# Expert 0's working memory at the other end of SBUF, a hand-given order for all engines from the end of attention on, Sinkhorn steps issued in thirds, and three of x's differences on GpSimd

## The chip, the core and the metric

The kernel runs on one core of a Trainium2 chip. The metric is the device time of one execution in microseconds; the median of three runs is given. Names of engines: PE is TensorE, DVE is VectorE, ACT is ScalarE, POOL is GpSimd, SP the queue from which all transfers here are issued.

## What is computed

Sliding-window attention with four sink positions, then a mixture of experts whose weights P come from a Sinkhorn normalisation over all tokens (cut from the reference):

```python
keep = is_sink | in_window                       # 4 sinks, window 128, B=4, H=8, S=768, D=64
a = softmax(where(keep, scale * q @ k.T, -1e9)); x = (a @ v) as (3072, 512)

logits = x @ w_gate; logits = logits - logits.max(); P = np.exp(logits)      # 3072 x 8
for _ in range(8):
    P /= P.sum(1, keepdims=True) + 1e-09
    P /= P.sum(0, keepdims=True) + 1e-09
    P *= N / E
for e in range(E):                               # E = 8, x 512 wide, hidden 1024
    out += P[:, e:e + 1] * (np.maximum(x @ w1[e], 0.0) @ w2[e])
```

## The kernel before

Every float32 operand of a large product is held as two pieces, a rounded one (made by ACT) and the rest (made by DVE from the raw value and the rounded one); a product is then three matmuls. `split` and `piece` make such pairs.

**Attention** (to about 322 us) runs over 48 units (batch, block of 128 tokens, half of the heads). Its PE order is written by hand; the order of the other engines is the scheduler's. In the gaps PE works on expert 0 for the first 1024 tokens (`plain`, L614, called through `run_fill`): one step of it is half of a first product (six 256-column matmuls, L587) or a third of a second product (three 512-column matmuls, L603). 36 of its 128 steps are left when attention ends. x goes to DRAM as `xscr`.

**Between attention and the table-driven part.** The remaining 36 steps are issued (L692 to L696) with the first five calls of the generator `sinkhorn` (L22) between them. Each of its eight iterations has a DVE part (row sums, reciprocal, multiplication, column sums), a small PE product that adds the column sums over the partitions (L49) and another DVE part. Then x's four blocks of 512 tokens by 256 columns are loaded (`load_x`, L917), four differences T1 to T4 of blocks are formed (`make_form`, L928, all four on DVE here) and split; then come the weight units of experts 1 to 7, numbered n, each 256 hidden columns wide (28 in all). A unit has seven first products M1 to M7 (`first`, six matmuls each, L721) and, one unit later, eight second products (`second`, six matmuls each, L993), in the order `STEPS`, where `S_` is a second product:

```python
STEPS = ["M2", "M1", "M5", S_, "M3", S_, "M6", S_, S_, "M7", S_, S_, "M4", S_, S_]
```

For a unit the raw weights r1 and r2 are loaded, sums of r1 formed on POOL (`sums1`, L781), and r1, the sums and r2 split into W1f and W2f; all of it goes to DRAM too, for the other two thirds of the tokens.

**What sets the order.** Units 0 to 2 (`AUTO = 3`) are left to the scheduler, with Sinkhorn's steps at high priority between them; from unit 3 on a table (`plan`) says at which step every engine's work stands. When Sinkhorn is done, expert 0's eight results are multiplied by its weights on DVE (L1013). The buffers of r1 and r2 (`rawp0`) lie where expert 0's work lay: its pools `wa`, `rawp` and `hp` share one end of SBUF with the attention's, and the next pools of that end follow when they close.

After unit 27 two more passes over the other tokens follow, from the stored pieces; they are not touched.

Of the kernel before, what the change touches and what calls it, by code (L numbers as in the profile page):

```python
# [16 lines left out]
P = 128  # L17
# [4 lines left out]
def sinkhorn(nc, pool, psum, Lt, Pt, ident, ones, NT, E, N):  # L22

    Lf = Lt.rearrange("p t e -> p (t e)")
    Pf = Pt.rearrange("p t e -> p (t e)")
    m1 = pool.tile([P, 1], F32, name="m1")
    nc.vector.reduce_max(m1, Lf, axis=AX.X)
# [10 lines left out]
    nc.scalar.activation(Pf, Lf, AF.Exp, bias=nm)  # L38
    for _ in range(8):
        r = pool.tile([P, NT], F32, name="rsum")  # L40
        nc.vector.reduce_sum(r, Pt, axis=AX.X)
        nc.vector.tensor_scalar(r, r, 1e-9, None, op0=ALU.add)
        nc.vector.reciprocal(r, r)
        nc.vector.tensor_tensor(Pt, Pt, r.unsqueeze(2).broadcast_to([P, NT, E]), op=ALU.mult)
        c = pool.tile([P, E], F32, name="csum")
        nc.vector.reduce_sum(c, Pt.rearrange("p t e -> p e t"), axis=AX.X)
        yield
        cb = psum([P, E])
        nc.tensor.matmul(cb, lhsT=ones, rhs=c, start=True, stop=True)  # L49
        c2 = pool.tile([P, E], F32, name="csum2")  # L50
        nc.vector.tensor_scalar(c2, cb, 1e-9, None, op0=ALU.add)
        nc.vector.reciprocal(c2, c2)
        nc.vector.scalar_tensor_tensor(Pt, Pt, float(N / E), c2.unsqueeze(1).broadcast_to([P, NT, E]), op0=ALU.mult, op1=ALU.mult)

# [25 lines left out]
def tile_any_span(ctx: ExitStack, tc: tile.TileContext, q, k, v, span, wg, w1, w2, out):  # L80
# [82 lines left out]
    with ExitStack() as ph:  # L163
# [5 lines left out]
        Lt = gp.tile([P, NT, E], F32, name="g_lt")  # L169
        Pt = gp.tile([P, NT, E], F32, name="g_pt2")  # L170
        for t in range(NT):
# [49 lines left out]
def tile_sink_attention_moe(ctx: ExitStack, tc: tile.TileContext, q, k, v, wg, w1, w2, out):  # L221
# [86 lines left out]
    Lt = const.tile([P, NT, E], F32, name="Lt")  # L308
    Pt = const.tile([P, NT, E], F32, name="Pt")
# [38 lines left out]
    with ExitStack() as ph:  # L348
        psg1 = ph.enter_context(tc.tile_pool(name="psg1", bufs=1, space=PSUM))
        pso1 = ph.enter_context(tc.tile_pool(name="pso1", bufs=1, space=PSUM))  # L350
        ps_s = ph.enter_context(tc.tile_pool(name="ps_s", bufs=2, space=PSUM))
        ps_t = ph.enter_context(tc.tile_pool(name="ps_t", bufs=2, space=PSUM))
        ps_o = ph.enter_context(tc.tile_pool(name="ps_o", bufs=2, space=PSUM))
# [3 lines left out]
        XF["B12"] = wa.tile([P, 2, KH, HT], F32R, name="B12", bufs=1)  # L357
        ab = ph.enter_context(ExitStack())
        att = ab.enter_context(tc.tile_pool(name="att", bufs=2))
        att1 = ab.enter_context(tc.tile_pool(name="att1", bufs=1))  # L360

        SS = []
        for j in range(2):
            s = att1.tile([P, SK], F32R, name=f"SS{j}")
            nc.vector.tensor_copy(s, zero[:, 0:SK])
            SS.append(s)

        KT = []
        for hh in range(2):
            t = att1.tile([P, 2, NP, (NB + 1) * SEG], F32R, name=f"KT{hh}")  # L370
            for w in range(2):
                for pr in range(NP):
                    nc.vector.tensor_copy(t[:, w, pr, SINK:SEG], zero)
            KT.append(t)

        units = [(b, i, hh) for b in range(B) for i in range(NB) for hh in range(2)]
        us = {}
        seq = {}
        raws = {}
        later, gates = [], []  # L380
# [48 lines left out]
        def split_v(n):  # L429
# [6 lines left out]
            if i == 0:  # L436
                split_sinks(b, hh)
# [60 lines left out]
        def values(n, pr):  # L498
# [15 lines left out]
            if pr == NP - 1:  # L514
                store_x(n)
# [921 lines left out]
```

## Time and profile before

| | us |
|---|---|
| median of 3 runs | 2194.5 (2192.27 to 2194.94) |
| the profiled execution | 2192.53, its span 2190.8 |
| PE busy in the span | 2152.2 (98%) |
| DVE, ACT, POOL busy | 1564.5, 888.4, 739.6 |
| mean granted clock of TensorE, as a share of full speed | 0.996 |

The page puts 93% of the span's chain of waits on PE. Busy time is counted in modelled matmul spans, so what a stretch is worth is read from how many matmuls it finished and at which granted clock (1.00 is 2.4 GHz, 0.50 is 1.2 GHz). The stretch that the change touches lies between 322 us (end of attention) and 421 us (first step of unit 3).

### The profile page before, as it was taken

The numbers are of one execution on the slowest core, as the hardware profiler recorded it, in microseconds if no ns is written. First come the engines' busy times: TensorE is split into PE (matmuls) and PEld (weight loads), VectorE is DVE, ScalarE is ACT, GpSimd is POOL, SyncE is SP. The second block draws the span as 40 slices with busy tenths as digits, with TensorE's granted clock in tenths as the row PEclk, the third lists the DMA queues.
The fourth block names the chain that finished last, engine by engine and source line by source line (L and its number), as shares of the span: only waits on it lengthen the run. The fifth ranks groups of instructions, "written<-read, shape, count | busy, mean of one in ns | idle before, by whom it ended". The sixth has DMA issues, their size and how long they took to land.

```text
span 2190.8 us, 31969 instructions
## 1 busy us (share of the span) xinstructions
PE 2152.2 (98%) x10525; PEld 1776.9 (81%) x10525; DVE 1564.5 (71%) x2913; ACT 888.4 (41%) x1906; POOL 739.6 (34%) x957
## 2 busy tenths in 40 slices
PE   7999998999999999999999999999999999999998
PEld 5888886788888888878888888888788888888886
DVE  8878868777778777776666666666756666666666
ACT  7777753344444444433333322233342333323222
POOL 7655542232332332232223332222322222332322
PEclk9999998999999999999999999999999999999999
DMA  7333324689988998876666666667866666666662
GB/s 175 83 84 87 81 76 149 199 294 289 315 294 289 308 305 288 279 274 220 193 201 202 199 201 202 201 193 231 310 211 201 203 199 193 202 205 192 202 194 82
DMA packets 396636, 454.89 MB, mean 208 GB/s; under 512 B 99696, under 2 KB 263728, under 8 KB 395568
## 3 DMA queue, kind: packets, MB, share of 16 engines
q1 hardware_dynamic: 396464, 452.77, 66.0%
q8 instruction: 86, 1.41, 0.3%
q14 instruction: 86, 0.70, 0.1%
HBM read 315.21 MB, written 137.46 MB: 207 GB/s over the span
## 4 chain that ended last, share of the span: by engine, by line
PE 93%; DVE 4%; ACT 1%; issue 1%; POOL 0%; DMA 0%; SPq 0%; DVEq 0%; POOLq 0%; ACTq 0%
PE c L721 39%; PE o L1284 20%; PE held L1284 8%; PE o L993 7%; PE held L993 7%; PE O L513 3%; PE ps L456 2%; PE g L587 2%; PE pt L477 2%; PE o L603 1%; PE pt L417 1%; PE O L603 1%; ACT sc L462 1%; PE ps L587 0%; PE O L543 0%
## 5 line engine op out<-in xcount | busy, mean ns | idle before, releaser
L747 ACT CAST hf<-w 128x512 fp32r<-128x512 f32 x448 | 265.7, 621 | 564.2 <-POOL w L1251 301.1
L1284 PE MATMUL o<-hf,W2q 128*128 128x512 f32 x1920 | 476.2, 392 | 0.1
L1284 PEld LDWEIGHTS o<-hf,W2q 128*128 128x128 f32 x1920 | 360.5, 188 | 78.1 <-DVE acc L1295 0.5
L721 PE MATMUL c<-T,W1q 128*128 128x512 f32 x1530 | 388.6, 389 | 0.0
L748 DVE TENSOR_TENSOR hf<-w,hf 128x512 fp32r<-128x512 f32 x448 | 330.2, 765 | 71.0 <-ACT hf L747 62.6
L721 PEld LDWEIGHTS c<-T,W1q 128*128 128x128 f32 x1530 | 287.0, 188 | 60.9 <-ACT M L1228 0.4
L1295 DVE TENSOR_TENSOR acc<-o,acc 128x512 f32<-128x512 f32 x300 | 206.3, 688 | 176.5 <-PE o L1284 176.1
L721 PE MATMUL c<-B,W1q 128*128 128x512 f32 x1134 | 278.5, 390 | 0.0
L1251 POOL TENSOR_TENSOR w<-w 128x512 f32<-128x512 f32 x64 | 83.1, 1298 | 500.9 <-DVE w L1233 492.3
L721 PEld LDWEIGHTS c<-B,W1q 128*128 128x128 f32 x1134 | 212.6, 188 | 44.8
L1232 DVE TENSOR_TENSOR w<-c,M 128x512 f32<-128x512 f32 x192 | 132.3, 689 | 143.0 <-PE c L721 138.4
L1228 ACT COPY M<-c 128x512 f32<-128x512 f32 x192 | 112.7, 587 | 252.9 <-PE c L721 252.2
L1284 PE MATMUL held<-hf,W2q 128*128 128x512 f32 x768 | 196.5, 392 | 0.0
L721 PE MATMUL c<-T,W1f 128*128 128x512 f32 x672 | 173.2, 394 | 0.4 <-DVE C L965 0.4
L993 PE MATMUL o<-W2f,h 128*128 128x512 f32 x672 | 171.5, 391 | 0.8 <-DVE acc L1000 0.8
L993 PE MATMUL held<-W2f,h 128*128 128x512 f32 x672 | 172.0, 390 | 0.0
L1284 PEld LDWEIGHTS held<-hf,W2q 128*128 128x128 f32 x768 | 144.2, 188 | 30.7
L1266 POOL TENSOR_TENSOR w<-w 128x512 f32<-128x512 f32 x64 | 105.6, 1650 | 177.6 <-DVE hf L748 177.6
L721 PEld LDWEIGHTS c<-T,W1f 128*128 128x128 f32 x672 | 127.1, 190 | 28.9 <-DVE C L965 1.2
L993 PEld LDWEIGHTS o<-W2f,h 128*128 128x128 f32 x672 | 126.1, 188 | 28.6 <-DVE acc L1000 1.2
L993 PEld LDWEIGHTS held<-W2f,h 128*128 128x128 f32 x672 | 126.1, 188 | 26.5
L1255 POOL TENSOR_TENSOR w<-w 128x512 f32<-128x512 f32 x64 | 83.7, 1308 | 176.0 <-DVE w L1233 174.6
(198 smaller groups left out, 3081.3 us busy)
## 6 DMA issues: line engine op xcount, KB each, us to landing
W2q<-w2s SPq DMA_DIRECT2D x448, 256.0 KB
W1q<-w1s SPq DMA_DIRECT2D x444, 256.0 KB
w1s<-W1f SPq DMA_DIRECT2D x56, 896.0 KB
w2s<-WT SPq DMA_DIRECT2D x136, 256.0 KB
r<-in_moe_w_dram SPq DMA_DIRECT2D x64, 512.0 KB
w2s<-W2f SPq DMA_DIRECT2D x56, 256.0 KB
PB<-psd SPq DMA_DIRECT2D x16, 512.0 KB
w2s<-W2f SPq DMA_DIRECT2D x56, 128.0 KB
```

Source lines behind the costliest of these rows:

```text
L513: nc.tensor.matmul(u["O"][:, pr], lhsT=x_, rhs=y_, start=(j == 0), stop=(j == len(ops) - 1))
L721: nc.tensor.matmul(ps, lhsT=w1(a, k), rhs=x[:, b, k, :], start=(start and j == 0), stop=(stop and j == len(TERMS) - 1), skip_group_check=n ...
L747: nc.scalar.copy(dst[:, 0], src)
L748: at(1, lambda: nc.vector.tensor_sub(dst[:, 1], src, f32(dst[:, 0])))
L993: nc.tensor.matmul(o, lhsT=h[c, th][:, a, off:off + P], rhs=W2F[n][:, w, c, :], start=(begin and c == 0 and j == 0), stop=(end and c == 1 ...
L1228: nc.scalar.copy(t, T["c2"])
L1232: nc.vector.tensor_add(w, T["c1"], T[m])
L1251: nc.gpsimd.tensor_sub(S3, T["A11"], T["A21"])
L1255: nc.gpsimd.tensor_add(T["A21"], T["A21"], T["A22"])
L1266: at(k, lambda: nc.gpsimd.tensor_sub(T["A11"], w, T["A11"]))
L1284: nc.tensor.matmul(o, lhsT=W2Q[part, n, m][:, a, k * P:(k + 1) * P], rhs=F[part, n, H_OF[m]][:, w, :], start=(j == 0 and (begin or not hol ...
L1295: nc.vector.tensor_add(sums[m, k], o, sums[m, k])
```

## The change

1. **Memory.** Expert 0's buffers (hidden values, second weights, x's block B12, first weights and raw weights) are taken from the right end of SBUF, attention's from the left. The left pools for units 0 and on are opened at once when attention ends, and wait tile by tile. Unit n's odd hidden values and all W2f continue in expert 0's buffers. x's block (1,0) is loaded into B12's.
2. **Order.** From the end of attention on, all engines stand in the order of a table: 28 steps (`REST`), each with one step of expert 0, then the units from 0 on, `plan` now with rows for units 0 to 2. The last eight steps of expert 0 are the `S_` of unit 0. Unit 0's second products take the held banks first. The second pieces of w2 of units 0 to 2 that were loaded again later (`job_w2`) are made in units 1 and 2.
3. **Sinkhorn.** An iteration is three calls instead of one; the additions of 1e-9 (two DVE instructions in each iteration) are replaced by an extra column and row of the tile that hold 1e-9. The rows of the table place the 27 calls: 13 in REST, 6 in unit 0, 8 in unit 1.
4. **Engines.** T1, T3 and T4 are formed on POOL (T2 on DVE); expert 0's results are weighted on ACT.

Loads at the end of attention on SP, before and after (x10 is block (1,0); r1 and r2 are raw weights of units in order):

```order
L527 DMA xscr_121<-xr_5239 128x4x128
L922 DMA x10_5599<-xscr_121 128x2x512
L922 DMA x00_5601<-xscr_121 128x2x512
L922 DMA x01_5603<-xscr_121 128x2x512
L922 DMA x11_5605<-xscr_121 128x2x512
L770 DMA r1_5635<-in_moe_w1_dram 128x4x256
L775 DMA r2_5637<-in_moe_w2_dram 128x2x512
L770 DMA r1_5824<-in_moe_w1_dram 128x4x256
```

```order
L538 DMA xscr_120<-xr_5244 128x4x128
L921 DMA x00_5351<-xscr_120 128x2x512
L921 DMA x01_5353<-xscr_120 128x2x512
L775 DMA r1_5355<-in_moe_w1_dram 128x4x256
L921 DMA x11_5357<-xscr_120 128x2x512
L780 DMA r2_5359<-in_moe_w2_dram 128x2x512
L775 DMA r1_5361<-in_moe_w1_dram 128x4x256
L775 DMA r1_5595<-in_moe_w1_dram 128x4x256
L921 DMA B12_5632<-xscr_120 128x2x512
```

The first raw weights stand between x's blocks, and block (1,0) has moved behind three units' r1, into B12's buffer.

PE where expert 0's steps end and unit 0 begins, before and after (ps and O are expert 0's first and second products, csum goes into a Sinkhorn product, c1 and c2 are unit 0's):

```order
L603 MATMUL O_5526<-W2_3793,h0_5397 128x512 x6
L49 MATMUL pt_5533<-csum_5488,ones_74 128x8
L603 MATMUL O_5526<-W2_3803,h1_5454 128x512 x6
L49 MATMUL o_5671<-csum_5544,ones_74 128x8
L721 MATMUL c2_5662<-B21_125,W1f_5644 128x512 x4
L721 MATMUL c1_5684<-B11_124,W1f_5644 128x512 x4
L721 MATMUL c2_5662<-B21_125,W1f_5644 128x512 x2
L49 MATMUL o_5695<-csum_5682,ones_74 128x8
L721 MATMUL c1_5684<-B11_124,W1f_5644 128x512 x2
```

```order
L56 MATMUL pt_5573<-csum_5538,ones_74 128x8
L598 MATMUL ps_5579<-B12_156,W1_3805 128x256 x2
L598 MATMUL ps_5579<-B22_125,W1_3805 128x256 x2
L598 MATMUL ps_5579<-B12_156,W1_3805 128x256 x2
L614 MATMUL O_5550<-W2f_3808,h11_5404 128x512 x3
L598 MATMUL ps_5579<-B22_125,W1_3805 128x256 x2
L598 MATMUL ps_5579<-B12_156,W1_3805 128x256 x2
L598 MATMUL ps_5579<-B22_125,W1_3805 128x256 x2
L614 MATMUL O_5550<-W2f_3808,h11_5404 128x512 x3
L725 MATMUL c2_5634<-B21_124,W1f_5448 128x512 x6
L56 MATMUL held1_5643<-csum_5606,ones_74 128x8
L725 MATMUL c1_5648<-B11_123,W1f_5448 128x512 x6
```

Expert 0 has eight steps left when unit 0 begins, and a Sinkhorn product stands at fixed places in PE's queue.

DVE at the same place, before and after (T and W1f rows make the rest pieces, rsum, csum and the Pt or Xt rows are Sinkhorn's, h is a hidden value's rest piece, acc a result of expert 0):

```order
L342 TENSOR_TENSOR T1_5609<-x00_5601,T1_5609 128x2x256
L51 TENSOR_SCALAR csum2_5673<-o_5671 128x8
L342 TENSOR_TENSOR T3_5616<-x01_5603,T3_5616 128x2x256
L52 RECIPROCAL csum2_5673<-csum2_5673 128x8
L342 TENSOR_TENSOR T3_5616<-x01_5603,T3_5616 128x2x256
L53 SCALAR_TENSOR_TENSOR Pt_120<-Pt_120,csum2_5673 128x192
L342 TENSOR_TENSOR T2_5623<-x11_5605,T2_5623 128x2x256
L41 TENSOR_REDUCE rsum_5677<-Pt_120 128x24
L342 TENSOR_TENSOR T2_5623<-x11_5605,T2_5623 128x2x256
```

```order
L752 TENSOR_TENSOR T2_5548<-x11_5357,T2_5548 128x2x256 x2
L604 SCALAR_TENSOR_TENSOR h01_5540<-ps_5541,h01_5540 128x256
L58 RECIPROCAL csum2_5575<-pt_5573 128x8
L59 SCALAR_TENSOR_TENSOR Xt_119<-Xt_119,csum2_5575 128x24x8
L752 TENSOR_TENSOR W1f_5448<-ST_5447,W1f_5448 128x512 x2
L48 TENSOR_REDUCE rsum_5592<-Xt_119 128x24
L49 RECIPROCAL rsum_5592<-rsum_5592 128x24
L604 SCALAR_TENSOR_TENSOR h01_5540<-ps_5579,h01_5540 128x256
L51 TENSOR_TENSOR Xt_119<-Xt_119,rsum_5592 128x24x8
L53 TENSOR_REDUCE csum_5606<-Xt_119 128x8
L622 TENSOR_TENSOR acc_3724<-O_5550,acc_3724 128x512
```

Unit 0's W1f now stands on DVE among expert 0's last steps, and T3 and T4 behind unit 0's first products. The diff, cut to its core:

```diff
-def sinkhorn(nc, pool, psum, Lt, Pt, ident, ones, NT, E, N):
+def sinkhorn(nc, pool, psum, X, ident, ones, NT, E, N):
...
     for _ in range(8):
         r = pool.tile([P, NT], F32, name="rsum")
-        nc.vector.reduce_sum(r, Pt, axis=AX.X)
-        nc.vector.tensor_scalar(r, r, 1e-9, None, op0=ALU.add)
+        nc.vector.reduce_sum(r, X[:, 0:NT, :], axis=AX.X)
         nc.vector.reciprocal(r, r)
+        yield
         nc.vector.tensor_tensor(Pt, Pt, r.unsqueeze(2).broadcast_to([P, NT, E]), op=ALU.mult)
         c = pool.tile([P, E], F32, name="csum")
-        nc.vector.reduce_sum(c, Pt.rearrange("p t e -> p e t"), axis=AX.X)
+        nc.vector.reduce_sum(c, X[:, :, 0:E].rearrange("p t e -> p e t"), axis=AX.X)
         yield
         cb = psum([P, E])
         nc.tensor.matmul(cb, lhsT=ones, rhs=c, start=True, stop=True)
         c2 = pool.tile([P, E], F32, name="csum2")
-        nc.vector.tensor_scalar(c2, cb, 1e-9, None, op0=ALU.add)
-        nc.vector.reciprocal(c2, c2)
+        nc.vector.reciprocal(c2, cb)
...
+    p0r = ctx.enter_context(ExitStack())
+    right = lambda stack, name, bufs: stack.enter_context(tc.tile_pool(name=name, bufs=bufs, reuse_waits="tile", side="right"))
+    hpr, w2pr, b12p = right(p0r, "hpr", 1), right(p0r, "w2pr", 2), right(p0r, "b12", 1)
...
-        wa = ph.enter_context(tc.tile_pool(name="wa", bufs=2))
-        rawp = ph.enter_context(tc.tile_pool(name="rawp", bufs=2))
-        hp = ph.enter_context(tc.tile_pool(name="hp", bufs=2))
+    wa, rawp = right(ph, "wa", 2), right(ph, "rawp", 2)
...
-            for k_ in (2, 12, 10, 10, 8):
-                with tc.high_priority():
-                    next(sk)
-                run_fill(k_)
-            for _ in fill:
-                pass
...
         def sinkhorn_step():
-                    for t in range(TH):
-                        nc.vector.tensor_scalar(acc[t], acc[t], Pt[:, t, 0:1], None, op0=ALU.mult)
+            for k, t in enumerate((4, 6, 0, 2, 5, 7, 1, 3)):
+                at(k + 1, lambda t=t: nc.scalar.activation(acc[t], acc[t], AF.Copy, scale=Pt[:, t, 0:1]))
...
+        for j, ks in {0: (), 1: ((0, (0, 1, 4, 7, 10, 3)), (1, (5, 6, 8, 11, 12, 9)))}.get(n, ((n, (0, 1, 3, 6, 9, 5)),)):
...
+            todo[12 if n == 1 else 2].append(lambda: load2(n + 1))
...
+        if n < 2:
+            for k in ((1, 2, 3, 6, 7, 8), (0, 1, 1, 4, 5, 5, 8, 8))[n]:
+                todo[k].append(sinkhorn_step)
+        if n == 0:
+            form_steps(todo, {"T3": (4, 5), "T4": (7, 9)})
+            todo[0].append(lambda: load_x(0, (1, 0)))
+            todo[3].append(lambda: make_form("T4", nc.gpsimd))
...
+    REST = 28
+    load_x(0, (0, 0), (0, 1))
+    load1(0)
+    load_x(0, (1, 1))
+    load2(0)
+    load1(1)
+    for k in (0, 2, 4, 6, 10, 12, 13, 17, 19, 20, 24, 26, 27):
+        todo[k].append(sinkhorn_step)
+    for k, f in ((7, lambda: make_form("T1", nc.gpsimd)), (12, lambda: make_form("T3", nc.gpsimd)),
+                 (17, lambda: sums1(0)), (18, lambda: make_form("T2")), (23, lambda: sums1(1)),
...
+    form_steps(todo, {"T1": (14, 15), "T2": (21, 22)})
+    for k in range(REST):
+        tick(lambda: [f() for f in todo[k]], lambda: next(fill))
```

## Rows read from the trace of the kernel before

**Rows 1.** The page's busy times: us (share of span) and instructions of each engine.

```profile
PE 2152.2 (98%) x10525; PEld 1776.9 (81%) x10525; DVE 1564.5 (71%) x2913; ACT 888.4 (41%) x1906; POOL 739.6 (34%) x957
```

**Rows 2.** Stages: stretch, length; busy us (instructions) by engine; granted clock, DMA share, GB/s.

```profile
322.20:348.50 26.30, 26.30 (x158) 22.87 (x156) 16.22 (x41) 7.39 (x16) 0.00 (x0) 1.00 0.19 65
348.50:352.40 3.90, 0.56 (x3) 0.30 (x2) 3.87 (x11) 0.09 (x1) 0.00 (x0) 1.00 0.67 207
352.40:360.70 8.30, 3.96 (x9) 2.94 (x10) 8.30 (x13) 3.83 (x8) 8.11 (x8) 0.71 0.65 230
360.70:369.50 8.80, 8.12 (x20) 5.71 (x19) 6.68 (x17) 4.27 (x8) 0.03 (x1) 0.50 0.89 304
369.50:420.65 51.15, 47.48 (x207) 37.34 (x207) 40.36 (x77) 15.88 (x30) 11.06 (x12) 1.00 0.68 220
420.65:900.00 479.35, 479.35 (x2104) 394.81 (x2103) 360.88 (x549) 217.38 (x403) 151.88 (x184) 1.00 0.89 292
```

**Rows 3.** PE in order of time: start, us, instructions, count [idle before].

```profile
322.20 0.87 PE L587 MATMUL ps<-B,W 128*128 128x256 f32 x6
...
420.65 2.92 PE L721 MATMUL c<-B,W1f 128*128 128x512 f32 x12
```

**Rows 4.** Whom PE waited for, 322 to 421 us: total, times, longest.

```profile
PE c L721 <- DVE W1f L342: 3.8, 1, 3.8
PE o L49 <- DVE csum L46: 2.2, 1, 2.2
PE o L1022 <- DVE pe L1017: 2.1, 1, 2.1
```

**Rows 5.** Whom SP's queue waited for, 319 to 352 us.

```profile
SPq L770 <- DVE h L593: 20.3, 1, 20.3
```

**Rows 6.** SP in order of time: x's loads, first raw weights.

```profile
319.39 3.44 SPq L922 DMA_DIRECT2D x<-xscr  x4
348.73 0.37 SPq L770 DMA_DIRECT2D r<-in_moe_w_dram  x1
```

**Rows 7.** DVE in order of time: one Sinkhorn iteration with POOL idle.

```profile
339.71 0.42 DVE L593 SCALAR_TENSOR_TENSOR h<-ps,h 128x256 fp32r<-128x256 f32 x1 [1.86 <-ACT h L592]
340.06 0.17 DVE L51 TENSOR_SCALAR csum<-pt 128x8 f32<-128x8 f32 x1
340.26 0.20 DVE L52 RECIPROCAL csum<-csum 128x8 f32<-128x8 f32 x1
340.50 0.36 DVE L53 SCALAR_TENSOR_TENSOR Pt<-Pt,csum 128x192 f32<-128x192 f32 x1
340.89 0.35 DVE L41 TENSOR_REDUCE rsum<-Pt 128x24 f32<-128x192 f32 x1
...
341.49 0.30 DVE L43 RECIPROCAL rsum<-rsum 128x24 f32<-128x24 f32 x1
341.82 0.36 DVE L44 TENSOR_TENSOR Pt<-Pt,rsum 128x192 f32<-128x192 f32 x1
342.22 0.52 DVE L46 TENSOR_REDUCE csum<-Pt 128x8 f32<-128x192 f32 x1
```

**Rows 8.** DVE in order of time: four of x's differences, POOL idle.

```profile
328.20 1.89 DVE L932 TENSOR_TENSOR x<-x,x 128x512 f32<-128x512 f32 x3
...
331.62 0.68 DVE L932 TENSOR_TENSOR x<-x,x 128x512 f32<-128x512 f32 x1
```

**Rows 9.** DVE's groups by shape, 352.4 to 360.7 us, POOL busy: count, us, mean ns.

```profile
L342 DVE TENSOR_TENSOR T<-x,T 128x512 fp32r<-128x512 f32 x5 | 4.5, 898 | 0.0
L342 DVE TENSOR_TENSOR W1f<-r,W1f 128x512 fp32r<-128x512 f32 x1 | 1.2, 1207 | 0.0
L53 DVE SCALAR_TENSOR_TENSOR Pt<-Pt,csum 128x192 f32<-128x192 f32 x1 | 0.9, 884 | 0.0
L44 DVE TENSOR_TENSOR Pt<-Pt,rsum 128x192 f32<-128x192 f32 x1 | 0.9, 878 | 0.0
```

**Rows 10.** POOL in order of time: a later form's difference, two halves.

```profile
923.13 3.38 POOL L932 TENSOR_TENSOR x<-x,x 128x512 f32<-128x512 f32 x2 [1.23 <-DVE x L932]
```

More of the change, by code (lines that the diff above doesn't have):

```diff
@@ L542, in gate_tile, with gate_step, load_plain, plain_g1 @@
+    def gate_step():
+        if gates and next(gates[0], 0) == 0:
+            gates.pop(0)
+            gate_step()
+    def load_plain(e, u):
+        r1, r2 = load_raw(rawp, e, u)
+        W1 = wa.tile([P, 2, KC, UF], F32R, name="W1")
+        split(W1, r1)
+        W2 = w2pr.tile([P, 2, 2, DM], F32R, name="W2f")
+        split(W2, r2)
+        return W1, W2
+    def plain_g1(W, u, c, h, g, th):
+        ps = bank1([P, GH])
+        i = 0
+        for a, w in ((0, 0), (0, 1), (1, 0)):
             for kc in range(KC):
-                nc.tensor.matmul(lg, lhsT=xr[:, kc, :], rhs=wg_raw[:, kc, :], start=(kc == 0), stop=(kc == KC - 1))
@@ L708, in tile_sink_attention_moe @@
+    ab.close()
     early.close()
@@ L733, in at @@
     def at(steps, f):
+        assert steps > 0
         due.setdefault(clock[0] + steps, []).append(f)
@@ new lines, in store, with store_unit, small @@
+    def store(dst, i, src):
+        for w in range(2):
+            nc.sync.dma_start(dst[:, i:i + src.shape[2] // HD, w], f32(src[:, w]).rearrange("p (a c) -> p a c", c=HD))
+    def store_unit(n):
+        e, u = units0[n]
+        kept(e, u)
+        store(w1s[e, u], 0, W1F[n].rearrange("p w a k f -> p w (a k f)"))
+        store(w2s[e, u], 0, W2F[n][:, :, 0, 0:HD])
+        store(w2s[e, u], 1, W2F[n][:, :, 1])
+    def small(n_):
+        return wtp.tile([P, 2, 2 * HD], F32R, name="WT")[:, :, 0:n_]
@@ new lines, in jobs, with load_x @@
+    def jobs():
+        units = [job_unit(0, u) for u in range(NU)]
+        xs = [job_x(2, q) for q in range(4)]
+        for j in range(NU):
+            yield from units[j]
+            yield from xs[j]
+    raw = {}
+    def load_x(part, *blocks):
+        for kh, th in blocks:
+            r = raw[f"B{kh + 1}{th + 1}"] = xraw(f"x{kh}{th}")
+            t0 = part * NPART + th * HT
+            nc.sync.dma_start(r, xscr[kh * KH:(kh + 1) * KH, :, t0:t0 + HT].rearrange("k p t -> p k t"))
+    PLACE = {"T1": "B11", "T3": "B12", "T2": "B22", "T4": "B21"}
@@ new lines, in tile_sink_attention_moe, with second, then @@
+    TILES = list(range(TH // 2, TH)) + list(range(TH // 2))
+    held = {}
+    def second(n, h):
+        e, u = units0[n]
+        for t in sorted(TILES, key=lambda t: n == 0 and t % 2 == 0):
+            th, off = divmod(t * P, HT)
+            hold = t % 2 == 1
+            if not hold:
+                o = ps0.tile([P, DM], F32, name="o", bufs=2)
+            elif u == 0:
+                o = held[t] = ps0.tile([P, DM], F32, name=f"held{t}")
+            else:
+                o = held[t]
+            begin, end = not hold or u == 0, not hold or u == NU - 1
+            for c in range(2):
+                for j, (a, w) in enumerate(((0, 0), (0, 1), (1, 0))):
+                    nc.tensor.matmul(o, lhsT=h[c, th][:, a, off:off + P], rhs=W2F[n][:, w, c, :],
+                                     start=(begin and c == 0 and j == 0), stop=(end and c == 1 and j == 2),
+                                     skip_group_check=hold)
+            def then(t=t, o=o, end=end):
+                if end:
+                    assert weighted
+                    nc.vector.scalar_tensor_tensor(acc[t], o, Pt[:, t, e:e + 1], acc[t], op0=ALU.mult, op1=ALU.add)
+                if n == len(units0) - 1:
+                    nc.sync.dma_start(out[t * P:(t + 1) * P, :], acc[t])
+            yield then
@@ L1153, in tile_sink_attention_moe @@
+    assert next(fill, 0) == 0
+    for k in (16, 17):
+        for f in todo[k]:
+            at(k - len(STEPS), f)
+    last_second = second(len(units0) - 1, hs[len(units0) - 1])
+    p0.close()
     with ExitStack() as p1:
```

1164 lines of the change are left out of this document (539 added, 625 removed).

## Prediction

> **What bounds the kernel now.** First the page's busy times: PE is busy 98% of the span [rows 1], so a gain can only lie where PE waits or runs slowly. The windows by stage show where that is [rows 2]: before 348.5 us and after 420.65 us PE is busy without a gap at clock 1.00; from 348.5 to 369.5 us it is busy 12.6 of 21.0 us, at clock 0.71 and then 0.50 for most of that, and from there to 420.65 us it idles another 3.7 us.
>
> How much that costs I read from the matmuls, since busy time at half clock is also loss. From the first step behind attention at 322.20 us to the first product of unit 3 at 420.65 us [rows 3] pass 98.45 us. In them lie the 36 left steps of expert 0 (26.3 us, no gap [rows 2]) and units 0 to 2: 42 + 90 + 90 = 222 matmuls. The undisturbed stage runs 2104 recorded matmuls in 479.35 us, 0.228 us each [rows 2], so 222 take 50.6 us; I add 0.9 us, an estimate, for the few small products. Undisturbed: 77.8 us. **Lost: 20.7 us.** No edit outside this stretch touches a wait of PE that the trace shows, so 20.7 us is the most that can come back.
>
> The cause is a chain. x is loaded at 319.39 us, but the first raw weights are issued at 348.73 us [rows 6], since their buffer lies where expert 0's hidden values still are: SP waited 20.3 us for those [rows 5]. All of unit 0's casts, sums and splits then come at once, with T's splits and Sinkhorn on DVE, which is busy 8.30 of 8.30 us [rows 2]; PE waits for DVE 3.8, 2.2 and 2.1 us [rows 4]. With PE nearly idle from 348.5 us the granted clock falls to 1.2 GHz and stays there until about 369 us [rows 2].
>
> **The change part by part.** *Loads.* The raw weights now go to memory that attention frees, in the queue between x's blocks. At 292 GB/s [rows 2] 512 KB take 1.8 us, so r1, third in the queue, lands at about 326 us and the sixth load at about 331 us. Unit 0 starts at 322.2 + 28 x 0.70 + 0.6 = 342.4 us. These loads are covered by expert 0's steps with 11 us to spare; without that cover they would cost what they cost now. Block (1,0) waits for expert 0's last read of B12, at about 341 us, and is needed as T4 in unit 0's twelfth step, 12 us later: 2 us of load and 3.4 us for its difference on POOL [rows 10] fit.
>
> *DVE* is what is late next, as the products, T's and Sinkhorn all pass it. Prices, start to start, with POOL idle: a 128x512 difference or split 0.60 us ((1.89 - 0.68) / 2, each 0.68 long [rows 8]), one of 128x256 0.35 us, Sinkhorn's thirds (the two additions of 1e-9 gone) 0.38 + 0.33 = 0.71, 0.40 + 0.5 = 0.9 and 0.24 + 0.39 = 0.63 us [rows 7]. From the new order of DVE:
> - 28 steps: Sinkhorn 0.9 for the maximum, three iterations and two thirds, 8.3 together; eight h splits 2.8; four acc 2.4; W1f 2.1; T1, T2 and one difference 3.6. Sum 20.1 us, against 20.2 us of PE.
> - Unit 0: six thirds 4.5; seven C and h 4.2; T3 and T4 2.4; unit 1's W1f 2.1; two acc 1.2. Sum 14.4 us, against 42 x 0.228 + 8 x 0.70 + 0.3 = 15.5 us.
> - Unit 1: seven thirds 5.1; C and h 4.2; W2f of two units 2.4; w2's sums and kept pieces 3.6; W1f 2.1; four acc 2.6. Sum 20.0 us, against 20.9 us.
>
> So DVE has 54.5 us of work for 56.6 us of PE, in one queue, with every Sinkhorn product standing in PE's queue behind its csum. That is too full to hide all. Walking the two queues against each other with these prices, PE waits at the csum ahead of expert 0's last four steps (about 0.4 us), at the csum behind unit 0's first product (1.1), at M4 of unit 0, whose T4 rest stands behind the sum of M7 on DVE (1.7), and at unit 1's first second product for W2f (0.6): **about 4 us** with POOL silent.
>
> *POOL* is not silent. In 352.4 to 360.7 us it is busy 8.11 us [rows 2], and DVE's instructions with two operands in SBUF are longer: five T splits 0.90 for 0.68, one of W1f 1.21 for 0.68, Sinkhorn's 0.88 for 0.36 twice [rows 7 to 9]. That is 1.1 + 0.5 + 1.0 = 2.6 us for 8.1 us of POOL, 0.33 us each. In the new stretch POOL has six halves of differences at 1.7 us [rows 10] and the sums of four units and two w2, 20 instructions at 1.0 us (8.11 / 8 [rows 2]): 30 us. At 0.33 this adds 10 us to DVE; but of its work there only half has two SBUF operands, where in the measured stretch it was nearly all, so I take 6 us, of which about 3 reach PE (the first POOL work meets DVE while it still waits for Sinkhorn's maximum). **Sum of the waits: 4 + 3 = 7 us.** Bounds: 2 us if the walk's small gaps are filled, 14 us if all 10 us reach PE.
>
> The Trainium skill, in "SBUF — State Buffer", section "Who interferes with whom", says that a VectorE instruction with two SBUF inputs and a GpSimd instruction that reads SBUF exclude each other, the second to issue blocking fully; it speaks against moving the differences to GpSimd. [Rows 9] agree in direction, and what the full rule would make of the sum is the third rival.
>
> *No cost:* weighting expert 0's results moves to ACT, busy 15.88 of 51.15 us in this stretch [rows 2]. The kept pieces moved into units 1 and 2 are in the DVE sums; dropping their second loads takes transfers from a stage at DMA share 0.89 [rows 2] in which PE never waited for one. Attention keeps its order.
>
> **Sum.** 2192.53 (the profiled execution) - 20.7 + 7 = 2178.8 us. That execution lies 2 us under the median and the runs spread over 2.7 us; I set the forecast 0.7 us higher, at **2179.5 us**.
>
> **The rivals.**
> - *DVE keeps up* (waits of 3 us or less). For it: in the first stage DVE is busy 16.22 of 26.3 us and still had T's work in it [rows 2]; against it: the 54.5 of 56.6 us. Time: 2192.5 - 20.7 + 2 to 3 = 2174 to 2175 us.
> - *A late transfer takes the wait's place.* r2 of unit 2 is issued only at step 12 of unit 1, some 4 us ahead of its cast, behind the stores of units 0 and 1 (about 7 MB, 25 us at 292 GB/s [rows 2], which start some 20 us earlier). ACT's cast would hold the copy of unit 2's M2, and so M5: 1 to 3 us. Time: 2181 to 2183 us.
> - *GpSimd shuts DVE out.* If each of POOL's instructions keeps a two-operand DVE instruction waiting for its whole length, DVE gets 30 us more, about 28 of them on the path: 4 + 28 = 32 us of waits, 2192.5 - 20.7 + 32 = 2204 us, slower than before. It decides from 0.57 us per us of POOL on (17 of 30); [rows 9] show 0.33. A weaker form ends within 0.2%: PE waits so often that the clock falls to 1.2 GHz again as from 352 us on [rows 2], some 10 us more at 222 matmuls' pace.
> - *The change doesn't do what it says:* the early loads still wait for something of expert 0. Its pools lie at the other end now, so I see nothing; it would be 2192 to 2195 us.
>
> **How the numbers follow.** Forecast (waits of 4 to 11 us, 2175.5 to 2183 us) 0.58; DVE keeps up 0.17; late transfer 0.10; blocked by GpSimd 0.11, of which about 0.05 ends slower, 0.04 within 0.2% and 0.02 a little faster; no effect 0.04, within 0.2%. 0.2% of 2194.5 is 4.4 us, about what a measurement can tell from no change. Faster: 0.58 + 0.17 + 0.10 + 0.02 = 0.87; same 0.08; slower 0.05. The range: waits of 2 us give 2173.8, waits of 14 us 2185.8; with the spread of the runs **2173.5 to 2187 us**.
>
> **What would show it.** In the changed kernel's windows PE should finish 322 to unit 3's start in 80 to 90 us, clock 1.00 throughout; the first r1 should be issued before 322 us. PE's waits should name DVE (csum, T4, W2f), each under 3 us, and DVE be busy over 90% from 330 to 380 us. The forecast is wrong if PE waits for a transfer or for POOL there, if the clock falls, or if two-operand DVE instructions beside POOL are no longer than alone (then the time is nearer 2174), or by more than 0.57 us per us of POOL.

## The result, and the profile after

The changed kernel takes 2202.7 us (median of 6 runs, 2201.4 to 2204.0); the kernel before, run beside it, 2193.25 us (2190.7 to 2194.9). The ratio is 1.0045, 95% interval 1.0032 to 1.0058: **slower by 0.45%**, where 2179.5 us were forecast, and outside the range.

The page's busy times answer [rows 1]:

```profile
PE 2170.2 (99%) x10525; PEld 1774.1 (81%) x10525; DVE 1561.5 (71%) x2888; ACT 893.1 (41%) x1914; POOL 742.5 (34%) x963
```

PE runs the same 10525 matmuls as before and is now busy 99% of the span instead of 98%. It idles less, and still needs longer: the modelled busy time grew by 18 us for the same work.

Where attention ends and where unit 3 begins, PE in order of time (start, us, ..., count), first before, then after:

```profile
317.68 0.28 PE L513 MATMUL O<-PS,VS 80*128 80x256 f32 x1
```

```profile
319.17 0.28 PE L524 MATMUL O<-PS,VS 80*128 80x256 f32 x1
...
411.39 2.91 PE L725 MATMUL c<-B,W1f 128*128 128x512 f32 x12
```

Unit 3's first product is PE's 2788th matmul in both kernels, so it marks equal work. From attention's last product to it pass 102.97 us before (317.68 to 420.65 [rows 3]) and 92.22 us after: **10.75 us are won in the stretch that the prediction speaks of.** Attention ended 1.5 us later; that differs from run to run (experiments 2 and 8, the same up to there, ended it at 317.93 and 319.07 us).

The rest is lost behind unit 3. From there to the end pass 1770.15 us before (2190.8 - 420.65) and 1789.51 us after (2200.9 - 411.39), **19.4 us more**, where the trace shows no new wait of PE (its listed waits there are 3.9 us in all, against 4.3 before). Windows from 1000 to 1500 us, in the passes that the change doesn't touch, columns as in [rows 2], first before, then after:

```profile
1000.00:1500.00 500.00, 500.00 (x2197) 412.25 (x2196) 336.67 (x496) 151.98 (x263) 145.49 (x105) 1.00 0.65 200
```

```profile
1000.00:1500.00 500.00, 500.00 (x2172) 407.43 (x2171) 333.61 (x490) 151.43 (x261) 143.56 (x104) 1.00 0.65 198
```

PE is busy without a gap in both, the clock is 1.00 in both, the DMA share is the same, and yet 25 products fewer are done: 230.2 ns a product instead of 227.6. Which products are slower shows in PE's order of time, first before, then after (`o` and `held` are second products, from hf and W2q; `c` first ones, from B or T and W1q):

```profile
1008.14 1.52 PE L721 MATMUL c<-T,W1q 128*128 128x512 f32 x6
...
1010.87 1.52 PE L721 MATMUL c<-B,W1q 128*128 128x512 f32 x6
1012.23 1.54 PE L1284 MATMUL o<-hf,W2q 128*128 128x512 f32 x6
1013.61 0.61 PE L721 MATMUL c<-T,W1q 128*128 128x512 f32 x2
```

```profile
1008.26 1.53 PE L725 MATMUL c<-B,W1q 128*128 128x512 f32 x6
1009.63 1.56 PE L1296 MATMUL o<-hf,W2q 128*128 128x512 f32 x6
1011.03 1.53 PE L725 MATMUL c<-T,W1q 128*128 128x512 f32 x6
```

Read from start to start: six first products take 1.36 us before (1010.87 to 1012.23) and 1.37 after; six second products 1.38 before (1012.23 to 1013.61) and 1.40 after (1009.63 to 1011.03). The view's own "us" hides this, since ends of matmuls are modelled. Over all records between 1000 and 1500 us, the starts of second products that follow one another are 229.3 ns apart before and 232.7 after, and those of first products 226.7 and 227.2; the first product ahead of a change to a second one took 225.8 ns before and 235.0 after.

The code of these products is the same. What the change moved is where their operands lie (addresses as the two kernels allocate them, in bytes of a partition). Lt and Pt, 1536 bytes, became Xt, 900 bytes (928 with the rounding); the small pool they are in lies at the low end of SBUF, called the left end here, and the tiles of these passes behind it moved down by 608 bytes: B11 from byte 4128 to 3520, and with it T, W1q and hf. The quarters of W2 (W2q) hang from the other end and stayed. Write x for the start of a product's moving operand (512 columns, here hf) and w for its stationary one (128 columns, here W2q). Modulo 256 W2q stands at 224 in both kernels, the left tiles at 32 before and at 192 after, so w - x went from 192 to 32.

### The profile page after: what moved, and what is told of

It is laid out like the page before. It is cut to its first block, busy times and chain, and to the rows that moved or that the text cites. A ratio compares the mean times of both kernels' runs of the same rounds, so it can differ in the third digit from the quotient of the medians.

```text
span 2200.9 us, 31963 instructions
## 1 busy us (share of the span) xinstructions
PE 2170.2 (99%) x10525; PEld 1774.1 (81%) x10525; DVE 1561.5 (71%) x2888; ACT 893.1 (41%) x1914; POOL 742.5 (34%) x963
## 4 chain that ended last, share of the span: by engine, by line
PE 92%; DVE 4%; ACT 2%; issue 1%; POOL 1%; DMA 0%; SPq 0%; DVEq 0%; ACTq 0%; POOLq 0%
PE c L725 39%; PE o L1296 20%; PE held L1296 8%; PE o L993 7%; PE held L993 7%; PE O L524 3%; PE ps L467 2%; PE g L598 2%; PE pt L488 2%; PE o L614 1%; PE pt L428 1%; ACT sc L473 1%; DVE T L752 0%; PE O L554 0%; DVE PT L351 0%
## 5 line engine op out<-in xcount | busy, mean ns | idle before, releaser
L1296 PE MATMUL o<-hf,W2q 128*128 128x512 f32 x1920 | 483.5, 395 | 0.0
L1263 POOL TENSOR_TENSOR w<-w 128x512 f32<-128x512 f32 x64 | 83.2, 1300 | 513.2 <-DVE w L1245 508.0
L1278 POOL TENSOR_TENSOR w<-w 128x512 f32<-128x512 f32 x64 | 105.7, 1652 | 177.7 <-DVE hf L752 177.7
L814 POOL TENSOR_TENSOR r<-r 128x256 f32<-128x256 f32 x28 | 20.7, 740 | 397.1 <-ACT M L956 236.1
```

The source lines that it names most:

```text
L1263: nc.gpsimd.tensor_sub(S3, T["A11"], T["A21"])
L1278: at(k, lambda: nc.gpsimd.tensor_sub(T["A11"], w, T["A11"]))
L1296: nc.tensor.matmul(o, lhsT=W2Q[part, n, m][:, a, k * P:(k + 1) * P], rhs=F[part, n, H_OF[m]][:, w, :], start=(j == 0 and (begin or not hol ...
```

## The experiments

The theory: TensorE's time per product depends on how the two operands' addresses stand to each other. The rivals: the new order, or the distance of tiles in SBUF, slows PE; or the absolute alignment of a tile does.

**1 and 2. The changed kernel with an unused tile behind Xt**, of 96 bytes and of 32 bytes per partition:

```diff
     Xt = const.tile([P, NT + 1, E + 1], F32, name="Xt")
+    const.tile([P, 24], F32, name="pad")     # experiment 2: [P, 8]
```

> The changed kernel with 96 unused bytes per partition behind Xt, so that every tile that follows at the left end starts 96 bytes higher (B11 at byte 3616 instead of 3520) and stands modulo 128 where it stood in the kernel before (32). Order and work are the changed kernel's. Theory A (TensorE's time per product depends on how the addresses of the two operands stand to each other modulo a small power of two): the stretch from unit 3's first product to the end goes back from 1789.5 us to the 1770 us that it takes before, 500 us hold about 2196 products instead of 2172, and the time is 2202.7 - 19.5 = 2183 us. Rival B (the new order on the engines, or the place of tiles far apart in SBUF, slows TensorE): the time stays at 2202 us and 500 us hold 2172 products. Rival C (only the absolute alignment of tiles counts, and 64 bytes is the better one): slower than 2203 us or the same.

> The changed kernel with 32 unused bytes per partition behind Xt (B11 at 3552), so that the tiles at the left end (B, T, W1q, hf) stand at 96 modulo 128, where the quarters of W2 at the right end stand in both kernels. Theory A: every product takes what those have whose two operands stand alike, 226.7 ns from start to start, instead of 230.2 on the average after and 227.7 before: the stretch from unit 3 to the end is 1762 us, and the time is about 2175 us, under both kernels. Rival B (order, or far places): 2202 us. Rival C (only the absolute alignment of a tile counts): 2183 us at best, as where the left tiles stand at 32 modulo 128, since 96 and 32 are alike modulo 64.

With 96 bytes: 2186.6 us, ratio to before 0.9966 (0.9951 to 0.9980); with 32 bytes: **2172.4 us, ratio 0.9902 (0.9885 to 0.9918)**. An unused tile of 32 bytes makes the changed kernel 30 us faster. The windows, first with 96 bytes, then with 32:

```profile
1000.00:1500.00 500.00, 500.00 (x2197) 412.14 (x2196) 337.67 (x498) 152.24 (x262) 145.81 (x105) 1.00 0.65 200
```

```profile
1000.00:1500.00 500.00, 500.00 (x2207) 414.04 (x2206) 339.78 (x500) 151.66 (x261) 146.03 (x105) 1.00 0.66 201
```

The pace before comes back with 96 bytes, and with 32 every group runs alike: all starts are 226.7 ns apart. The order as the cause is out. With 96 bytes the time came out 3.6 us above the expectation, and the units behind unit 3 show why (450 to 900 us, before, then with 96 bytes):

```profile
450.00:900.00 450.00, 450.00 (x1975) 370.58 (x1974) 342.17 (x520) 203.95 (x378) 144.64 (x175) 1.00 0.91 299
```

```profile
450.00:900.00 450.00, 450.00 (x1955) 366.36 (x1955) 327.52 (x501) 197.63 (x366) 130.69 (x162) 1.00 0.85 283
```

20 products fewer, 4.6 us. Before, a unit's h and W2f lay at the same end, and stood alike modulo 256 (both at 32 or both at 224). The change puts all of W2f at the right end and every second unit's h at the left, so part 1 of the change pulls these operands apart as well; 32 bytes bring them together (1987 products in this window), 96 don't.

**3 and 4. The kernel before with the same tile**, of 32 and of 64 bytes behind Pt, nothing else changed:

```diff
     Pt = const.tile([P, NT, E], F32, name="Pt")
+    const.tile([P, 8], F32, name="pad")     # experiment 4: [P, 16]
```

> The kernel before with 32 unused bytes per partition behind Pt (B11 at 4160 instead of 4128) and nothing else changed: the left tiles stand at 64 modulo 128, as they do in the changed kernel. Theory A: the stretch from unit 3 to the end grows from 1770 to about 1789 us, and the time is about 2212 us, without any edit to the order. Rival B (the order is what slows TensorE): 2193 us.

> The kernel before with 64 unused bytes per partition behind Pt (B11 at 4192): the left tiles stand at 96 modulo 128, like the quarters of W2 at the right end. Theory A: all products at 226.7 ns, the stretch from unit 3 to the end 1762 us instead of 1770, and the time about 2185.5 us. Rival B: 2193 us. Rival D (only the offset modulo 64 counts, which is the same for all operands in the kernel before): 2193 us as well.

With 32 bytes the kernel before takes **2213.0 us**, ratio 1.0082 (1.0066 to 1.0099): the loss without any edit to the order. With 64 bytes it takes 2210.4 us, 1.0073 (1.0056 to 1.0090), and here the expectation of 2185.5 us was wrong: operands that agree modulo 128 and not modulo 256 are nearly as slow as those of experiment 3 (2168 products in 500 us against 2162). The windows, 32 bytes, then 64:

```profile
1000.00:1500.00 500.00, 500.00 (x2162) 405.85 (x2161) 331.87 (x487) 152.22 (x263) 144.79 (x104) 1.00 0.64 197
```

```profile
1000.00:1500.00 500.00, 500.00 (x2168) 407.34 (x2167) 332.47 (x488) 151.34 (x261) 143.25 (x103) 1.00 0.64 197
```

So the addresses decide, and the period is longer than 128 bytes. A tile's own alignment doesn't tell them apart: the left tiles stand at 96 modulo 128 in experiment 4 as in experiment 2, and the one is slow, the other fast.

**5 and 6. The period, and the order's own worth.** The changed kernel with 288 bytes (left tiles at 224 modulo 512, W2q at 480), and the kernel before with 448 bytes, the operands of experts 1 to 7 all alike:

> The changed kernel with 288 unused bytes behind Xt: the tiles at the left end stand at 224 modulo 512, the quarters of W2 at 480, so the two differ modulo 512 and agree modulo 256. The 32-byte pad made them agree modulo 512 (2172.4 us, 500 us hold 2207 products); the 64-byte pad in the kernel before made them agree only modulo 128, and helped nothing. If the period is 256 bytes: 2172 us and 2207 products. If it is 512 bytes: above 2180 us, and 500 us hold 2165 to 2197 products.

> The kernel before with 448 unused bytes behind Pt: the left tiles of experts 1 to 7 stand at 480 modulo 512, like the quarters of W2 at the right end. Order and work are those before. If the relative place modulo 512 is what counts: 2207 products in 500 us as with the 32-byte pad after, so some 8 us less behind unit 3 and a time of 2185 us; the difference to the 2172.4 us of the changed kernel with its 32-byte pad is then what the new order is worth with addresses out of the way, 12 to 14 us. If something else than the addresses made that kernel fast: 2193 us or more.

With 288 bytes after: 2173.0 us, ratio 0.9912 (0.9896 to 0.9929), 2208 products in 500 us, so **the period is 256 bytes**. The kernel before with 448 bytes: 2182.7 us, ratio 0.9957 (0.9942 to 0.9971), 2207 products. Between these two only the change itself is left: 9.7 us of their medians, measured side by side, where 12 to 14 were expected. (Expert 0's operands lie alike in the first of the two only, but its 256-column products show no difference: their starts lie 118 to 119 ns apart, as a median, in both.) In their profiled executions attention's last product and unit 3's first stand, after with 288 bytes, then before with 448, at

```profile
318.21 0.29 PE L525 MATMUL O<-PS,VS 80*128 80x256 f32 x1
...
409.25 2.88 PE L726 MATMUL c<-B,W1f 128*128 128x512 f32 x12
```

```profile
318.24 0.28 PE L514 MATMUL O<-PS,VS 80*128 80x256 f32 x1
...
421.17 2.20 PE L722 MATMUL c<-B,W1f 128*128 128x512 f32 x9
```

91.0 against 102.9 us: in these two executions the change is worth 11.9 us in its stretch once addresses are out of the way. One execution of each says this only within some 2 us: the same stretch took 100.3 to 103.0 us in the four kernels with the order before (before, experiments 3, 4 and 6), and 90.8 to 92.2 us in the four with the changed one (after, experiments 1, 2 and 5).

**7. The cost by itself**: nothing but products of zeros, in series, with the two starts set by hand, in one execution:

```diff
+        a = SHIFT + x // 4 + 512 * (k % 3)
+        b = SHIFT + w // 4 + 128 * (k % 4)
+        return dict(out=c, lhsT=W[:, b:b + 128], rhs=X[:, a:a + 512], start=(k == 0), stop=(k == n - 1))
```

> Only products, no attention and no experts (nothing of the reference is computed): series of 60 products of 128 x 512, one behind the other, with nothing else running; the moving operand starts at x bytes and the stationary one at w bytes modulo 512, both otherwise moving on by multiples of 512. If the distance w - x modulo a power of two decides: x0w0 takes 226.7 ns a product, as do x96w96 and any other with equal places; x96w128 takes what x0w32 does, x96w160 what x0w64, x96w224 what x0w128, x96w352 what x0w256, x96w480 what x0w384, x32w480 what x0w448; x0w32, x0w64 and x0w128 above 229 ns; x0w256 at 226.7 if the period is 256 bytes. If it takes a second engine or a transfer to slow a product down: all series at 226.7 ns. In turns (six at w = 480 and six at w = 32, x = 32) and in pairs (six at 32 and 32, six at 96 and 96): above 226.7 ns, if changes from one place to another cost by themselves; the pairs at 226.7 ns if only a product's own two operands count.

PE in order of time; a group's name gives x and w, and 60 products lie between one start and the next (120 in turns and in pairs):

```profile
54.68 13.94 PE L36 MATMUL x0w0B<-X,W 128*128 128x512 f32 x60
68.68 14.27 PE L39 MATMUL x0w32B<-X,W 128*128 128x512 f32 x60
...
111.69 14.27 PE L48 MATMUL x0w128B<-X,W 128*128 128x512 f32 x60
...
140.33 14.02 PE L54 MATMUL x0w192B<-X,W 128*128 128x512 f32 x60
154.41 14.27 PE L57 MATMUL x0w224B<-X,W 128*128 128x512 f32 x60
168.74 13.91 PE L60 MATMUL x0w256B<-X,W 128*128 128x512 f32 x60
...
282.76 13.89 PE L84 MATMUL x96w96B<-X,W 128*128 128x512 f32 x60
296.71 14.27 PE L87 MATMUL x96w128B<-X,W 128*128 128x512 f32 x60
...
339.67 13.90 PE L96 MATMUL x96w352B<-X,W 128*128 128x512 f32 x60
...
381.99 27.62 PE L105 MATMUL turnsB<-X,W 128*128 128x512 f32 x120
409.66 27.94 PE L108 MATMUL pairsB<-X,W 128*128 128x512 f32 x120
```

What counts is w - x modulo 256: 0 and 256 are alike, at x = 0 and at x = 96; 192 lies a little above; all others lie together. The series begin with up to 16 products that settle; the last 39 starts of a series are 226.7 ns apart at w - x = 0, 228.9 at 192, 233.3 to 233.4 at 32, 64, 128, 160 and 224 and 234.3 at 96. One series doesn't fit: x96w480, at 128 modulo 256, takes 232.2, where it was expected to take what x0w384 does (233.4). It takes no second engine and no transfer: products alone slow each other (from 54 us to the end of the series the DMA share is 0.00 and no other engine works). That the streaming of one product meets the weight load of the next is the likely reading; it isn't shown. In pairs, where each product's two operands stand alike but both move by 64 bytes every six products, the starts are 230.6 ns apart after the first 20, so that change of place costs by itself. In turns, the pattern of the kernel before (w - x of 192 and 0, six and six), they are 227.7 apart, the mean of the two series (228.9 and 226.7) and nearly what that kernel has (227.8): there the change itself costs nothing that shows.

The Trainium skill, in "TensorE: Matmul & The Clock Gate", section "Step-by-step: what each phase is for", says that loading the next tile's weights doesn't steal read bandwidth from the running matmul, as the two operands have ports of their own. Between 226.7 and 234.3 ns in this run, with the place of the two operands as the only difference, speaks against that for these products, though no run shows that it is the weight loads that take the time; the measurement decides.

**8. POOL's share**: the changed kernel with 32 bytes and the three differences formed on DVE.

```diff
-    for k, f in ((7, lambda: make_form("T1", nc.gpsimd)), (12, lambda: make_form("T3", nc.gpsimd)),
+    for k, f in ((7, lambda: make_form("T1", nc.vector)), (12, lambda: make_form("T3", nc.vector)),
...
-            todo[3].append(lambda: make_form("T4", nc.gpsimd))
+            todo[3].append(lambda: make_form("T4", nc.vector))
```

> The changed kernel with its 32-byte pad (2172.4 us) and T1, T3 and T4 formed on DVE instead of POOL, the order otherwise kept: DVE gets six instructions more, at 0.6 us each alone 3.6 us, and POOL loses six of about 1.7 us, 10 us. By the prediction's price (POOL lengthens DVE by 0.33 us per us, so these cost DVE 3.4 us where they are): the same time within 1 us. If POOL shuts DVE out for the whole length of its instructions: about 5 us faster (2167 us). If POOL's work beside DVE costs next to nothing: 2 to 4 us slower (2174.5 to 2176.5 us), with longer waits of PE for csum.

2172.9 us, ratio 0.9912 (0.9896 to 0.9929): the same time as experiment 2, and as experiment 5 measured beside it (2173.0 us). Windows of the stretch, with the differences on POOL (experiment 2), then on DVE:

```profile
325.00:412.00 87.00, 83.50 (x390) 66.61 (x389) 72.57 (x139) 41.35 (x80) 29.80 (x32) 0.98 0.64 215
```

```profile
325.00:412.00 87.00, 82.34 (x395) 65.98 (x394) 75.14 (x146) 40.83 (x79) 20.53 (x26) 1.00 0.64 218
```

POOL has 9.27 us less and DVE 2.57 us more, though it got six instructions of 0.68 us [rows 8], 4.1 us. So these 9.27 us of POOL had cost DVE some 1.5 us, 0.16 us each: an estimate from the two rows, and far from the 0.57 from which the third rival decides. The rule from the Trainium skill that the prediction weighed ("SBUF — State Buffer", section "Who interferes with whom"), taken in full, would have made this kernel some 5 us faster; it isn't. These runs don't tell where PE would stand without the sums' POOL work. And the same time is made of two parts: PE's waits from 320 to 425 us are 4.7 us against 3.3 in experiment 2, the longest for csum 1.4 instead of 0.7, while the clock didn't fall behind the wait for C, as it did there (1.00 against 0.98 in the windows above, some 1.7 us). So the differences may cost 1 to 2 us more on DVE than on POOL.

**9. The longest wait**, ahead of M4 of unit 0: two of the table's steps moved, with 32 bytes.

```diff
-            for k in ((1, 2, 3, 6, 7, 8), (0, 1, 1, 4, 5, 5, 8, 8))[n]:
+            for k in ((1, 2, 3, 6, 7, 10), (0, 1, 1, 4, 5, 5, 8, 8))[n]:
...
-            form_steps(todo, {"T3": (4, 5), "T4": (7, 9)})
+            form_steps(todo, {"T3": (4, 5), "T4": (6, 9)})
```

> The changed kernel with its 32-byte pad and two of the table's steps moved: T4's first rest piece at unit 0's step 6 instead of 7 (into a gap of DVE of 0.7 us), and the third of Sinkhorn that ends in csum at step 10 instead of 8, so that the sum C behind M7 stands 1.5 us of DVE work earlier. With the 32-byte pad alone PE waits 1.6 us for that C ahead of M4, and the clock falls to 1.2 GHz for about 4 us behind it. If that wait is DVE's order: it shrinks to about 0.8 us, the clock stays at 1.00, and the time falls by 1 to 3 us, to 2169.5 to 2171.5 us. If csum becomes late instead: PE waits for csum behind unit 1's first product, and the time stays at 2172 us or above.

2172.2 us (2171.9 to 2172.6), ratio 0.9902 (0.9886 to 0.9919): no gain that shows, where 1 to 3 us were expected. Whom PE waited for, 320 to 425 us (total, times, longest):

```profile
PE pt L56 <- DVE csum L53: 1.1, 2, 0.7
PE held L994 <- DVE W2f L753: 0.8, 1, 0.8
...
PE c L726 <- DVE C L965: 0.2, 1, 0.2
```

The wait for C went from 1.6 to 0.2 us, and a wait for W2f of 0.8 us took part of its place; unit 3 begins 1.8 us earlier behind attention than in experiment 2. The profiled execution then lost that at 921 us, where the clock fell behind a pause that both kernels have (experiment 2, then this one):

```profile
925.00:930.00 5.00, 5.00 (x24) 4.14 (x23) 3.94 (x6) 1.70 (x3) 0.00 (x0) 1.00 0.38 142
```

```profile
925.00:930.00 5.00, 5.00 (x20) 4.04 (x19) 3.35 (x6) 1.38 (x3) 0.00 (x0) 0.83 0.05 18
```

**10. Sinkhorn not in thirds**, with 32 bytes:

```diff
-    for k in (0, 2, 4, 6, 10, 12, 13, 17, 19, 20, 24, 26, 27):
+    for k in (0, 2, 4, 6, 12, 12, 12, 18, 18, 18, 25, 25, 25):
...
-            for k in ((1, 2, 3, 6, 7, 8), (0, 1, 1, 4, 5, 5, 8, 8))[n]:
+            for k in ((2, 2, 2, 7, 7, 7), (1, 1, 1, 5, 5, 5, 8, 8))[n]:
```

> The changed kernel with its 32-byte pad and Sinkhorn no longer issued in thirds: the PE product of one iteration and the DVE work up to the next csum (0.63 + 0.71 + 0.9 = 2.2 us alone) are one call, at steps 12, 18 and 25 of the remaining steps, 2 and 7 of unit 0, 1 and 5 of unit 1; instructions and work are the same. With the 32-byte pad and thirds: 2172.4 us, PE waits 3.3 us between 320 and 425 us. If DVE's queue is as full as the prediction has it (54.5 of 56.6 us), a block of 2.2 us in it holds up the hidden values and C behind it: PE's waits in that stretch grow by 2 to 6 us, they name DVE h, C or W2f, and the time is 2174.5 to 2178.5 us. If DVE has room where it counts: 2172 to 2173 us, and the thirds are worth nothing by themselves.

2175.8 us, ratio 0.9924 (0.9908 to 0.9941): 3.4 us above experiment 2 by the medians, with intervals that still overlap. PE's waits, 320 to 425 us:

```profile
PE c L726 <- DVE C L965: 3.0, 2, 2.4
PE ps L599 <- DVE h L605: 1.1, 1, 1.1
```

They name C and h, the work behind Sinkhorn's block, as a full DVE queue would have it. But all waits there together are 4.7 us against 3.3 in experiment 2, 1.4 more where 2 to 6 were expected, and unit 3 begins 1.4 us later behind attention. The rest of the 3.4 us lies behind unit 3, where in this profiled execution the clock fell behind the pause at 921 us as in experiment 9 (0.66 from 925 to 930 us). The kernel without thirds is slower: its fastest run, 2175.0 us, lies above the slowest of experiments 2 and 5, 2174.0. That 1.4 us of this belong to the thirds is what the waits say; with the order in thirds the stretch itself differs by as much between executions (90.8 to 92.2 us), so the size isn't shown.

## Why the prediction was wrong, point by point

The sum gave 2178.8 us; the profiled execution took 2202.7. The 23.9 us between them are 19.4 us behind unit 3, 3.0 us in the stretch (10.75 won instead of 20.7 - 7 = 13.7) and 1.5 us in attention.

- **The step that failed** is the sentence on the bounds: "No edit outside this stretch touches a wait of PE that the trace shows, so 20.7 us is the most that can come back". It is true of waits, and the waits there didn't change. It took for granted that 0.228 us a product [rows 2] belongs to the products. That figure depends on where operands lie, and the diff's smallest line, a tile of 1536 bytes that became one of 900, moved every tile at the left end. Experiments 1 to 6 show it: with all operands alike the part behind unit 3 takes 1760.5 us in the changed order (experiment 5: 2169.8 - 409.25) and 1761.7 in the order before (experiment 6: 2182.9 - 421.17), so addresses cost the kernel before 8.4 us there and the changed one 29.0 us. No rival of the prediction had this; its slower one was GpSimd's.
- **Lost time, 20.7 us**: the stretch was the right one, and the chain behind it too. With the raw weights loaded early unit 0 begins at 347.02 us instead of 352.98, before, then after:

```profile
352.98 3.45 PE L721 MATMUL c<-B,W1f 128*128 128x512 f32 x8 [1.68 <-ACT W1f L341]
```

```profile
347.02 1.54 PE L725 MATMUL c<-B,W1f 128*128 128x512 f32 x6
```

- **Loads**: r1 is issued at 321.86 us, ahead of 322, and unit 0 starts without waiting for it; 342.4 us was forecast for that start, 4.6 us too early, of which 1.5 us are attention's and 1.8 us the two waits for csum below; 1.3 us no wait names. No transfer held PE up, so the second rival fell.

```profile
321.86 0.52 SPq L775 DMA_DIRECT2D r<-in_moe_w_dram  x1
```

- **DVE's waits, 4 us, and 3 us by POOL**: the trace names 4.1 us. That is the 4 us of the walk with POOL silent, not the 7 us of the sum with POOL at work, so the agreement is in part luck. Whom PE waited for in the changed kernel, 320 to 425 us, as in [rows 4]:

```profile
PE pt L56 <- DVE csum L53: 1.8, 2, 1.1
PE c L725 <- DVE C L964: 1.6, 1, 1.6
PE held L56 <- DVE csum L53: 0.5, 2, 0.3
PE c L725 <- ACT M L956: 0.2, 1, 0.2
```

  4.1 us, none over 3 us. The wait ahead of M4 was forecast at 1.7 us and is 1.6. But it hangs on C and not on T4's rest: M4 adds to c1, which C must have read first. The waits for csum are spread otherwise than forecast (PE in order of time):

```profile
337.80 0.39 PE L56 MATMUL pt<-csum,ones 128*128 128x8 f32 x2 [1.13 <-DVE csum L53]
...
343.88 0.39 PE L56 MATMUL pt<-csum,ones 128*128 128x8 f32 x2 [0.70 <-DVE csum L53]
...
348.84 0.39 PE L56 MATMUL held<-csum,ones 128*128 128x8 f32 x2 [0.27 <-DVE csum L53]
```

  The second, ahead of expert 0's last four steps, was forecast at 0.4 us; the third, behind unit 0's first product, at 1.1; the first, seven steps of expert 0 earlier, not at all. W2f's showed only in other executions (0.8 us in experiment 9). DVE is busy 44.48 us from 330 to 380 us, 89%, where over 90% was to show it.
- **POOL, 6 us on DVE**: for the differences the price holds, 0.16 us per us of POOL against the 0.2 of the sum (6 us for 30), and they cost the same within 1 to 2 us on either engine (experiment 8). The price of the sums, 20 us of POOL, and how much reached PE, was not measured apart.
- **What was lost beyond these waits** is 9.95 - 4.1 = 5.9 us. Of it 1.7 us are clock, since it was not 1.00 throughout, as forecast: behind the wait for C it fell (windows after; next to last three columns are granted clock, DMA share, GB/s):

```profile
362.00:364.00 2.00, 0.83 (x3) 0.50 (x4) 1.90 (x4) 0.98 (x2) 0.00 (x0) 1.00 0.00 0
364.00:366.00 2.00, 2.00 (x8) 1.54 (x6) 1.31 (x3) 1.09 (x4) 0.00 (x0) 0.65 0.00 0
366.00:368.00 2.00, 2.00 (x8) 1.62 (x6) 1.95 (x4) 1.52 (x3) 0.00 (x0) 0.50 0.69 196
```

  2 x 0.35 + 2 x 0.5 = 1.7 us at full clock. Experiment 5, with the same wait for C and the same fall, takes 1.2 us less (91.04 against 92.22); 0.6 of this are shorter waits (3.5 us in all against 4.1), so the slower products cost about half a us here. The last 3.7 us no listed wait names. The starts of all records show most of them from unit 0 on: behind 13 products, most of which come right after a Sinkhorn product or a gap, the next one begins 75 to 120 ns late, 1.2 us together, and four gaps of 0.16 to 0.42 us, which the view leaves out, are 1.0 us more. So the "undisturbed" time, with 0.9 us for all small products, was set too low; the rest stays open.
- **The forecast with addresses left out** would have come out inside its range, though not at its centre: 2172.4 to 2173.0 us against 2182.7 us for the order alone is 9.7 to 10.3 us, and 11.9 us in the stretch of one pair of executions, where 13.7 were forecast.

## What to carry to other kernels

Before an edit that adds, removes or resizes a tile is costed by its waits, look at which tiles move with it: a pool's size sets the address of everything behind it. In a kernel that TensorE bounds, let the moving and the stationary operands of its 128 x 512 products stand alike modulo 256 bytes, those that hang from the other end of SBUF included, and measure it; here an unused tile of 32 bytes was worth 30 us in the changed kernel, three times the rest of the change, and one of 448 bytes 11 us in the kernel before (2182.7 against 2193.5 us). And compare the number of matmuls in equal stretches, or starts of equal groups: the busy share and the waits showed nothing of it.

## What the runs showed of the hardware

- The time of a 128 x 512 product of this kind is 226.7 ns where the two operands' addresses agree modulo 256 bytes, 228.9 ns where the stationary one stands 192 bytes on, and 232.2 to 234.3 ns elsewhere (experiment 7). Only products whose stationary operand has rows of 512 bytes and whose moving one has rows of 2048 were measured so; the starts of expert 0's 256-column products lie 118 to 119 ns apart, as a median, at w - x of 0 and of 32 alike (experiments 5 and 6). Why the period is 256 bytes was not found out.
- Groups that are each well placed can still lose where they alternate: 230.6 ns instead of 226.7 in groups of six whose two operands both stand at 32, then both at 96. Where only the stationary operand moved (w - x of 192 and 0 in turn), no such loss shows (227.7 ns, the mean of the two; both experiment 7).
- Whether a pause of PE of 1.6 to 1.9 us also costs clock differs from run to run: behind the 1.6 us wait for C the clock fell to 1.2 GHz in the changed kernel and in experiments 2 and 5, and stayed at 1.00 in experiments 1 and 8 (whose windows from 362 to 368 us show 1.00 throughout); behind the 1.9 us pause at 921 us it fell in experiments 9 and 10 and in 2 and 8 not. Differences of 1 to 2 us between kernels of this study may be no more than that.
